# Attention plus gated MLP on one core: two-pass output tiles for three chunks, GpSimd normalising six token tiles, 128-query units in the whole last chunk, 45 exponential slots

## The chip, the cores and the metric

The kernel runs on one core of a Trainium2 chip. The core has five engines with a queue each, every queue in order: TensorE (PE in the profile; its weight loads are PEld), VectorE (DVE), ScalarE (ACT), GpSimd (POOL) and SyncE (SP), which here only issues DMAs. The metric is the device time of one execution in microseconds, the median of several runs. Before the change it is 1200.54 us (three runs: 1199.99, 1200.54 and 1211.0).

## The reference

```python
x = A_x                                   # (1, 2048, 512) bf16
xn = layernorm(x)                         # no scale, no shift, eps 1e-5
q, k, v = split(xn @ wqkv)                # 32 heads of 16
p = softmax(q @ k.T / 4)                  # per head, 2048 x 2048
attn = (p @ v) @ wo
h = silu(xn @ w1) * (xn @ w3)             # 512 -> 1792
out = x + attn + h @ w2
```

There are 32 × 2048 × 2048 scores, 134 million. Each is computed twice in this kernel: once with queries on the partitions, for the maximum of its row, and once with keys on the partitions, for the exponential.

## The kernel before

**Tiling.** The 2048 queries are four chunks of 512 (`qc` 0 to 3), the 32 heads are eight groups of four (`g`). A pair (qc, g) is worked in units of queries: 256 each as a rule, `UNIT_HEAD = (128, 128, 256)` for the first pair, and four of 128 for each of the last four pairs (`NTAIL = 4`). A unit goes through these stages:

1. *Maximum.* For each 128 queries and each pair of heads and each 512 keys, TensorE writes two banks of 512 scores (L1037), and VectorE reduces the 1024 columns to two maxima (`tensor_reduce`, L1079). There are 1024 such reduces in the kernel, eight for 128 queries; banks 0 to 3 make two places for them, so at most two are under way.
2. *Final maximum.* GpSimd merges the partial maxima in six small steps (L1187 to L1194); for the first three and the last eight units VectorE does it in one (L1216). The negative maximum becomes two rows beside Q: in most units over a DMA transpose (L1210) and two small DMAs (L1206), in the first eight units and the last four pairs over two matmuls and an evacuation (`tile_QT2`, L796; `FAST_AUG`).
3. *Exponentials.* TensorE writes the transposed scores, 512 columns to a bank (L1303), and ScalarE writes exp to a slot of 512 columns in SBUF (`PT`, L1316; two banks at once at L1346). A unit of 256 queries takes 32 slots, one of 128 takes 16; `PT` has `NPT = 39`.
4. *Values.* `tile_PV` multiplies with V and a column of ones (L567), which frees the slots. ScalarE evacuates (`U`, L1411), and a chain normalises: DMA `Lc` (L1432), reciprocal on GpSimd (L1436), DMA to DRAM and back, broadcast (L1441, L1445), multiplication on GpSimd (L1456). One chain runs at a time, and PV of unit u waits for the chain of unit u−2 (`pv_ready`). The last three units (`FAST_PV`) take a reciprocal and a product on VectorE instead (L1401, L1403).

**MLP.** `ffn_pair` makes one slice of 128 of the 1792 hidden columns for one chunk: two matmul groups, three evacuations on ScalarE (L837, L839, L843), three operations on GpSimd (L821, L824, L826) into a slot of `hT`. There are 14 slices in a chunk, 56 in all; `NHT = 24` slots, whose first four hold V's weights until V is done, and the next 16 the normalised x until it is transposed. A slice waits until the slot it takes has been read.

**Output.** `tile_OUT` adds in one bank x (identity matmul), 14 products of `hT` with w2, and 8 of the attention output with wo. For chunks in `TWO_PASS` (only chunk 2) the 14 products make a tile of their own (`tile_OUTP`), evacuated to `osb` by ScalarE and added again through an identity matmul (`g_b`) in `tile_OUT`. The last chunk has its own pair of tiles, `tile_OUTA` and `tile_OUTB`.

**Head.** x is loaded in groups of two or four token tiles (of 128 tokens). A group's statistics are taken on VectorE or ScalarE (`STATS`), two small operations on GpSimd make 1/sigma (L621, L624), and the group is normalised by VectorE (L641) or ScalarE (L637, after a small product on VectorE, L629), as `NORM` says, one letter for each of seven groups: tiles 0-1, 2-3, 4-5, 6-7, 8-11, 12-13, 14-15. The letter "p" would give it to GpSimd (`poolq["nx"]`, L647). Then a transpose and an evacuation (L672) make `xnT`, and four tiles give K of the first group for 512 keys (L688).

**Order of the work.** A planner (`while True` at L1876) walks through all engines at build time, and always places the operation that by its own table of costs can start earliest, with rules for what TensorE takes next. Each engine then runs its list in that order; only semaphores hold it back on the chip. In `later_dma` a DMA is booked with 2.3 us to landing unless told otherwise; a normalisation on GpSimd is booked with 2.08 us (L647). `ffn_from` paces the MLP slices over the reduces (from reduce −60 to reduce 600 of 1024).

Of the kernel before, what the change touches and what calls it, by code (L numbers as in the profile page):

```python
# [6 lines left out]
BF16 = mybir.dt.bfloat16  # L7
# [235 lines left out]
def _c_act(n):  # L243
    return n / 1200.0 + 0.05
# [14 lines left out]
def _build(nc, A_x, A_wqkv, A_wo, B_w1, B_w3, B_w2, out):  # L259
# [33 lines left out]
    DMA_RATE = 360.0  # L293
    NOW = 2
    FAST_HEAD = 8
    FAST_TR = 896
    DVE_HEAD = 3
# [53 lines left out]
    def sb(name, shape, dt):  # L351
        return ctx.enter_context(nc.sbuf_tensor(name, list(shape), dt))

    with ctx:
        PT = sb("PT", [128, NPT, 512], BF16)
        x_sb = PT[:, 0:NT, :]
        xr = sb("xr", [128, NXR, D], BF16)
        osb = sb("osb", [128, 4, D], BF16)
        mv = sb("mv", [128, NT, 2], FP32)
        lnr = sb("lnr", [128, NT], FP32)  # L360
        lnb = sb("lnb", [128, NT], FP32)
# [95 lines left out]
        def later_dma(fn, reads, writes, lat=2.3, cb=None, pred=None, occ=0.62):  # L457
            spq.append(_Item(fn, reads, writes, occ, lat, cb, pred))
# [25 lines left out]
        LN_GROUPS = ((0, 2), (2, 4), (4, 6), (6, 8), (8, 12), (12, 14), (14, 16))  # L484
        XN_KEYS = [("hT", DC + t) for t in range(NT)]
        xn_sb = hT[:, DC:DC + NT, :]
        landed = [DMA_FIRST]
        kb_sum = [0]

# [260 lines left out]
        def tile_V(t, need=None):  # L750
            groups = []
            for c in range(DC):
                groups.append((lambda bk, c=c: all_groups(
                    bk, xnT[:, c, t * 128:(t + 1) * 128], wv[:, c, :], D,
                    start=c == 0, stop=c == DC - 1), WV_KEYS + [("xnT", t)], _c_mm(512), None))

            def evac(bk):
                return [_Item(lambda e: e.activation(Vaug[:, t, :, 0:16],  # L758
                                                     bank(bk).rearrange("p (h d) -> p h d", d=16), ACTF.Identity),
                              [("ps", bk)], [("V", t)], _c_act(512), cb=lambda op: done.add(("V", t)))]  # L760
            return _Tile("V%d" % t, groups, evac, need=need, pred=lambda: ("xnT", t) in done)

        ug_last = {}
# [46 lines left out]
        def ffn_pair(sc, fc):  # L810
# [47 lines left out]

            def start_g():
                if idx + 2 < NQC * FC:  # L860
# [9 lines left out]
        def g_x(tg, stop=False):  # L870
            return (lambda bk: all_groups(bk, ident[:, :], xr[:, tg % NXR, :], D, start=True, stop=False),
                    [("ident",), ("xr", tg % NXR)], _c_mm(512), None)

        def g_h(tg, fc, stop=False, start=False):
            qc, ts = divmod(tg, 4)
            hs = hslot(qc * FC + fc)
            return (lambda bk: all_groups(bk, hT[:, hs, ts * 128:(ts + 1) * 128], w2[:, fc, :], D,
                                          start=start, stop=stop),
                    [("hT", hs), ("w2",)], _c_mm(512), None)
# [6 lines left out]
                    lambda: ("ON", qc, g, ts) in done)  # L886

        def store(tg):
            later_dma(lambda e: e.dma_start(out_v[:, tg, :], osb[:, tg % 4, :]), [("osb", tg % 4)], [("out", tg)],
                      cb=lambda op: done.add(("ST", tg)))  # L890

        def tile_OUT(tg):
            qc, ts = divmod(tg, 4)
            two = qc in TWO_PASS
            groups = [g_x(tg)] + ([g_b(ts)] if two else [g_h(tg, fc) for fc in range(FC)])
            groups += [g_on(qc, ts, g, False, g == NG - 1) for g in range(NG)]

            def evac(bk):
                def cb(op):
                    store(tg)  # L900
                    done.add(("OUT", tg))
                    done.add(("HP", tg))
                    if tg + NXR < NT:
                        load_xr(tg + NXR)
                return [_Item(lambda e: e.activation(osb[:, tg % 4, :], bank(bk), ACTF.Identity),
                              [("ps", bk)], [("osb", tg % 4)], _c_act(512), cb=cb)]
            return _Tile("OUT%d" % tg, groups, evac, pred=lambda: ("xr", tg) in done
                         and (("HP", tg) in done if two else (tg < 4 or ("ST", tg - 4) in done)
                              and all(("hT", qc * FC + fc) in done for fc in range(FC)))
                         and all(("ON", qc, g, ts) in done for g in range(NG)), paced=True)  # L910

        def g_b(ts):
            return (lambda bk: all_groups(bk, ident[:, :], osb[:, ts, :], D, start=False, stop=False),
                    [("ident",), ("osb", ts)], _c_mm(512), None)

        def tile_OUTP(tg):
            qc, ts = divmod(tg, 4)
            groups = [g_h(tg, fc, fc == FC - 1, fc == 0) for fc in range(FC)]

            def evac(bk):  # L920
                return [_Item(lambda e: e.activation(osb[:, ts, :], bank(bk), ACTF.Identity),
                              [("ps", bk)], [("osb", ts)], _c_act(512), cb=lambda op: done.add(("HP", tg)))]
            return _Tile("OUTP%d" % tg, groups, evac, pred=lambda: (tg < 4 or ("ST", tg - 4) in done)
                         and all(("hT", qc * FC + fc) in done for fc in range(FC)), paced=P_PACED)

        def tile_OUTA(tg):
# [15 lines left out]
        def tile_OUTB(tg):  # L942
            qc, ts = divmod(tg, 4)
            groups = [g_on(qc, ts, g, g == NGA, g == NG - 1) for g in range(NGA, NG)]

            def evac(bk):
                def cb(op):
                    store(tg)
                    done.add(("OUT", tg))
                return [_Item(lambda e: e.tensor_tensor(osb[:, tg % 4, :], bank(bk), opart[ts], ALU.add),  # L950
                              [("ps", bk)] + OP_KEYS[ts], [("osb", tg % 4)], _c_dve(512), cb=cb)]
            return _Tile("OUTB%d" % tg, groups, evac, pred=lambda: ("OUTA", tg) in done and ("ST", tg - 4) in done)


        def split_rows(u):
# [306 lines left out]
        def p2_cand():  # L1262
# [27 lines left out]
            def emit():  # L1290
# [20 lines left out]
                def cb(op):  # L1311
# [2 lines left out]
                    exp_unit[u] += 1  # L1314
                    exp_emitted.add((u, kb, j))
                expq.append(_Item(lambda e: e.activation(PT[:, sl, :], bank(b), ACTF.Exp, scale=SCALE),  # L1316
                                  [("ps", b)], [("PT", sl)], _c_act(512), cb=cb, exp=(b, sl, (u, kb, j))))
            return st, emit, rd

        def exp_pair(x, y):  # L1320
# [19 lines left out]
            def cb(op):  # L1340
# [4 lines left out]
                n_pair[0] += 1  # L1345
            return _Item(lambda e: e.activation(PT[:, s0:s1 + 1:s1 - s0, :], ps8[:, b0:b1 + 1:b1 - b0, :], ACTF.Exp,  # L1346
                                                scale=SCALE),
                         [("ps", b0), ("ps", b1)], [("PT", s0), ("PT", s1)], _c_act(1024), cb=cb)
        n_pair = [0]


# [3 lines left out]
        def tile_PV(u):  # L1355
# [5 lines left out]
            for kt in range(NT):  # L1361
# [16 lines left out]
                    return f  # L1378

                def reads(kb=kb, kt=kt):  # L1380
                    return ([("V", kt), ("Vone",), ("ones_t",)] + [("PT", pt_slot[(u, kb, j)]) for j in range(4)])

                def gcb(kb=kb, i0=i0):
                    if i0 == kpb - 1:
# [33 lines left out]
        def nrm_next():  # L1418
# [11 lines left out]

            def n1(op=None):
                later_dma(lambda e: e.dma_start(Lc[:, pp, 0:nl], U[16:128:32, us, 0:nq]), [("U", us)], [("Lc", pp)],  # L1432
                          cb=n2)
# [5 lines left out]

            def n3(op):  # L1440
                later_dma(lambda e: e.dma_start(rd_[pp][0:4 * nq].rearrange("(p n) -> p n", n=nl), Rc[:, pp, 0:nl]),  # L1441
                          [("Rc", pp)], [("rd", pp)], cb=n4)

            def n4(op):
                later_dma(lambda e: e.dma_start(  # L1445
                    R[:, pp, 0:nq], rd_[pp][0:4 * nq].rearrange("(j q) -> j q", q=nq).unsqueeze(1)
                    .broadcast_to([4, 32, nq])), [("rd", pp)], RK, cb=n5)

            def n5(op):
                nrm_busy[0] = False  # L1450
# [506 lines left out]
```

## Time and profile before

| | |
|---|---|
| median of three runs | 1200.54 us |
| the profiled execution's own time | 1199.56 us |
| its span in the trace | 1197.8 us |
| TensorE clock granted | 0.999 |
| VectorE busy | 1180.1 us (99%) |
| ScalarE busy | 1174.2 us (98%) |
| TensorE busy | 1116.0 us (93%) |
| GpSimd busy | 439.9 us (37%) |

In the profile "L1079" is a line of the kernel, "part<-ps" says that the tile `part` is written and `ps` read. Busy is the union of the instructions' spans: an engine that pipelines looks full when its instructions overlap at their ends, so a busy share near 100% is not yet proof of a full engine. "Idle before" is how long the engine stood before the instructions of a group, and the name behind the arrow is what released it. The timeline merges equal neighbours: start, length, engine, line, operation, names, shapes, count.

### The profile page before, as it was taken

What the parts mean: (1) busy time and instruction counts of PE and PEld (TensorE: products, weight loads), DVE (VectorE), ACT (ScalarE), POOL (GpSimd) and SP (SyncE); (2) the same over time, 40 slices, a digit from 0 to 9 for tenths busy, and PEclk for the clock granted to TensorE, in tenths of its full rate; (3) what the DMA queues carried; (4) which work ended last, traced back from release to release, by engine and by line L of the source; (5) the groups of instructions that cost most, each with busy time, mean ns of one, the idle gap of its engine ahead of it and who ended that gap; (6) DMA issues with size and microseconds to landing.
All of it is one profiled execution on the core that took longest, in us unless ns stands there. A gap on an engine that the chain in (4) does not pass through costs nothing.

```text
span 1197.8 us, 32744 instructions
## 1 busy us (share of the span) xinstructions
PE 1116.0 (93%) x13564; PEld 467.9 (39%) x13731; DVE 1180.1 (99%) x1087; ACT 1174.2 (98%) x2272; POOL 439.9 (37%) x854
## 2 busy tenths in 40 slices
PE   8999999999999999998999999999999999889998
PEld 3433333333334433333333333433333343345554
DVE  8999999999999999999999999999999999999995
ACT  7899999999999999999999999999999999999997
POOL 2254555645222256642222243265632122233220
PEclk9999999999999999999999999999999999999999
DMA  6422223222001122210001121022100200000000
GB/s 185 124 59 72 52 64 81 48 55 52 19 23 29 41 54 50 61 29 20 22 16 33 31 59 29 22 64 45 40 20 20 59 22 19 18 18 14 12 12 23
DMA packets 128321, 51.41 MB, mean 43 GB/s; under 512 B 97252, under 2 KB 128172, under 8 KB 128172
## 3 DMA queue, kind: packets, MB, share of 16 engines
q1 hardware_dynamic: 128172, 49.30, 16.3%
q8 instruction: 108, 1.77, 0.6%
q14 instruction: 41, 0.34, 0.1%
HBM read 38.86 MB, written 6.74 MB: 38 GB/s over the span
## 4 chain that ended last, share of the span: by engine, by line
DVE 44%; ACT 27%; PE 25%; issue 3%; POOL 1%; DMA 1%; another core or an unknown queue 0%; POOLq 0%
DVE part L1079 43%; ACT PT L1316 19%; PE ps L581 9%; PE ps L1303 7%; PE ps L567 5%; PE ps L1037 4%; ACT PT L1346 3%; ACT th L837 1%; ACT zg L839 1%; ACT ub L843 1%; ACT U L1411 1%; ACT xnT L672 0%; ACT kq L743 0%; ACT Vaug L758 0%; DMA R<-rd 0%
## 5 line engine op out<-in xcount | busy, mean ns | idle before, releaser
L1079 DVE TENSOR_REDUCE part<-ps 128x2 f32<-128x1024 f32 x1024 | 1159.9, 1212 | 0.7 <-PE ps L1303 0.4
L1316 ACT ACTIVATE PT<-ps 128x512 bf16<-128x512 f32 x1750 | 922.4, 627 | 5.7 <-PE ps L1303 2.5
L1303 PE MATMUL ps<-QT,KT 32*128 32x256 bf16 (+1 forms) x4672 | 538.0, 259 | 11.7 <-ACT PT L1346 6.0
L1037 PE MATMUL ps<-KT,QT 32*128 32x512 bf16 x2048 | 400.7, 384 | 12.5 <-DVE part L1079 7.9
L1303 PEld LDWEIGHTS ps<-QT,KT 32*128 32x128 bf16 x4672 | 204.3, 92 | 224.8 <-issue 96.9
L581 PE MATMUL ps<-xnT,ident 128*128 128x512 bf16 (+1 forms) x599 | 174.6, 348 | 23.0 <-ACT PT L1346 7.0
L1436 POOL TENSOR_TENSOR Rc<-Lc,mone 128x8 f32<-128x8 f32 (+1 forms) x70 | 106.0, 1514 | 228.0 <-DMA Lc<-U 228.0
L567 PE MATMUL ps<-PT,Vaug 128*17 128x256 bf16 (+1 forms) x4672 | 175.2, 261 | 4.5 <-ACT zg L839 1.3
L581 PE MATMUL ps<-xnT,w 128*128 128x512 bf16 (+1 forms) x550 | 146.1, 334 | 13.0 <-ACT zg L839 5.7
L1346 ACT ACTIVATE PT<-ps 128x1024 bf16<-128x1024 f32 x149 | 151.7, 1050 | 0.8 <-PE ps L1303 0.5
L1037 PEld LDWEIGHTS ps<-KT,QT 32*128 32x128 bf16 x2048 | 98.1, 91 | 131.5 <-DVE part L1079 66.6
L567 PEld LDWEIGHTS ps<-PT,Vaug 128*17 128x17 bf16 x4672 | 86.5, 89 | 78.0 <-issue 57.6
L581 PEld LDWEIGHTS ps<-xnT,ident 128*128 128x128 bf16 x700 | 52.3, 97 | 107.7 <-ACT PT L1316 47.7
L824 POOL TENSOR_TENSOR a<-zg,ub 128x512 f32<-128x512 bf16 x56 | 64.6, 1153 | 44.7 <-ACT ub L843 44.3
L1187 POOL TENSOR_TENSOR mx<-part 128x16 f32<-128x16 f32 (+1 forms) x62 | 13.2, 212 | 179.1 <-DVE part L1079 179.0
L581 PEld LDWEIGHTS ps<-xnT,w 128*128 128x128 bf16 x578 | 44.2, 97 | 84.2 <-issue 47.0
L826 POOL TENSOR_TENSOR hT<-a,t 128x512 bf16<-128x512 f32 x56 | 71.0, 1269 | 2.6
L581 PE MATMUL ps<-w,hT 128*128 128x256 bf16 (+1 forms) x270 | 68.7, 336 | 2.6 <-issue 1.1
L1456 POOL TENSOR_TENSOR wk_on<-U,R 128x256 bf16<-128x256 f32 (+1 forms) x37 | 23.4, 632 | 118.0 <-DMA R<-rd 118.0
L1456 POOL TENSOR_TENSOR on_b<-U,R 128x256 bf16<-128x256 f32 (+1 forms) x33 | 23.4, 710 | 71.1 <-DMA R<-rd 71.1
L839 ACT ACTIVATE zg<-ps 128x512 bf16<-128x512 f32 x56 | 36.3, 649 | 0.0
L843 ACT ACTIVATE ub<-ps 128x512 bf16<-128x512 f32 x56 | 35.9, 641 | 0.0
(89 smaller groups left out, 520.8 us busy)
## 6 DMA issues: line engine op xcount, KB each, us to landing
w<-in_B_w_dram SPq DMA_DIRECT2D x112, 128.0 KB
R<-rd SPq DMA_DIRECT2D x55, 128.0 KB
QT<-qd SPq DMA_DIRECT2D x31, 128.0 KB
KT<-kd SPq DMA_DIRECT2D x28, 128.0 KB
xr<-in_A_x_dram SPq DMA_DIRECT2D x16, 128.0 KB
out_dram<-osb SPq DMA_DIRECT2D x16, 128.0 KB
qd<-kq SPq DMA_DIRECT2D x15, 128.0 KB
w<-in_B_w_dram SPq DMA_DIRECT2D x1, 1792.0 KB
```

The lines of the kernel that those rows point to most:

```text
L567: ins = e.matmul(bank(bk)[32 * i:32 * i + m, c0 + a:c0 + b], make_lhsT(i), rhs if (a, b) == (0, ncols) else rhs[:, a:b], start=start, stop ...
L581: return e.matmul(bank(bk)[0:rows, c0 + a:c0 + b], lhsT, rhs if (a, b) == (0, ncols) else rhs[:, a:b], start=start, stop=stop, **kw)
L824: q.append(_Item(lambda e: e.tensor_tensor(a32[:, :], zg[:, ss, :], ub[:, ss, :], ALU.mult), [("zg", ss), ("ub", ss)], [("a32",)], 1.1, 1.25))
L826: q.append(_Item(lambda e: e.tensor_tensor(hT[:, hslot(idx), :], a32[:, :], t1[:, :], ALU.mult), [("a32",), ("t1",)], [("hT", hslot(idx))] ...
L839: _Item(lambda e: e.activation(zg[:, ss, :], bank(bk), ACTF.Identity, scale=0.5), [("ps", bk)], [("zg", ss)], _c_act(512), cb=part_done, n ...
L843: return [_Item(lambda e: e.activation(ub[:, ss, :], bank(bk), ACTF.Identity), [("ps", bk)], [("ub", ss)], _c_act(512), cb=part_done)]
L1037: ins = e.matmul(bank(2 * sl + i), QT[32 * j:32 * j + 32, qs, q * 128:(q + 1) * 128], KT[32 * j:32 * j + 32, g, c_ * 512:(c_ + 1) * 512], ...
L1079: redq.append(_Item(lambda e: e.tensor_reduce(dst, pair_ap.rearrange("p (a b) -> p a b", b=512), AX.X, ALU.max), writes, [("part", par, qt ...
L1303: ins = e.matmul(bank(b)[:, i * nq:(i + 1) * nq], KT[32 * j:32 * j + 32, g, (k0 + i) * 128:(k0 + i + 1) * 128], QT[32 * j:32 * j + 32, qs, ...
L1316: expq.append(_Item(lambda e: e.activation(PT[:, sl, :], bank(b), ACTF.Exp, scale=SCALE), [("ps", b)], [("PT", sl)], _c_act(512), cb=cb, e ...
L1346: return _Item(lambda e: e.activation(PT[:, s0:s1 + 1:s1 - s0, :], ps8[:, b0:b1 + 1:b1 - b0, :], ACTF.Exp, scale=SCALE), [("ps", b0), ("ps ...
L1436: poolq["nrm"].append(_Item(lambda e: e.tensor_tensor(Rc[:, pp, 0:nl], Lc[:, pp, 0:nl], mone[:, 0:nl], ALU.pow), [("Lc", pp), ("mone",)], ...
```

## The change

Five edits come together.

1. `TWO_PASS = (0, 1, 2)`: the output tiles of chunks 0 and 1 are made in two passes as well. `osb`, the buffer of both passes, grows from 4 to 8 tiles (`NOSB`).
2. `hT` becomes a part of the same SBUF tensor as `PT`, with 20 slots in place of 24. The four that hold V's weights become exponential slots when V is done, beside `NPT = 41`: 45 in all in place of 39. The MLP keeps 16 slots, and a slice waits for the two-pass tile of the chunk that had its slot before.
3. `NORM`: tiles 8 to 11 go from VectorE to GpSimd, tiles 12 and 13 from ScalarE to GpSimd.
4. `NTAIL = 8`: all eight pairs of the last chunk are worked in units of 128 queries (before, the last four).
5. The planner books the three DMAs of the normalising chain with 2.6, 2.6 and 2.9 us in place of 2.3.

```diff
-    NPT = 39
+    NPT = 41
-    TWO_PASS = (2,)
+    TWO_PASS = (0, 1, 2)
-    NHT = 24
+    NHT = 20
-    NTAIL = 4
+    NTAIL = 8
+    NOSB = 8
+    LAT_L = 2.6
+    LAT_D = 2.6
+    LAT_R = 2.9
-    NORM = "dddddaa"
+    NORM = "ddddppa"
...
-        PT = sb("PT", [128, NPT, 512], BF16)
+        PT = sb("PT", [128, NPT + NHT, 512], BF16)
-        osb = sb("osb", [128, 4, D], BF16)
+        osb = sb("osb", [128, NOSB, D], BF16)
-        hT = sb("hT", [128, NHT, 512], BF16)
+        hT = PT[:, NPT:NPT + NHT, :]
...
+        def v_done(t):
+            done.add(("V", t))
+            if all(("V", t_) in done for t_ in range(NT)):
+                pt_free.extend(range(NPT, NPT + DC))
...
         def hslot(idx):
-            return (idx + DC) % NHT
+            return DC + idx % (NHT - DC)
...
                 if idx < NHT - DC:
                     return True
-                if idx < NHT:
-                    return all(("V", t) in done for t in range(NT))
-                return all(("HP", (idx - NHT) // FC * 4 + ts) in done for ts in range(4))
+                return all(("HP", (idx - NHT + DC) // FC * 4 + ts) in done for ts in range(4))
...
-            groups = [g_x(tg)] + ([g_b(ts)] if two else [g_h(tg, fc) for fc in range(FC)])
+            groups = [g_x(tg)] + ([g_b(tg)] if two else [g_h(tg, fc) for fc in range(FC)])
...
                 later_dma(lambda e: e.dma_start(Lc[:, pp, 0:nl], U[16:128:32, us, 0:nq]), [("U", us)], [("Lc", pp)],
-                          cb=n2)
+                          lat=LAT_L, cb=n2)
```

In the rest of the diff `osb` is indexed by `tg % NOSB` in place of `tg % 4` or `ts`, the keys of slots above `NPT` are those of `hT`, and the other two DMAs of the chain get `LAT_D` and `LAT_R`.

More of the change, by code (lines that the diff above doesn't have):

```diff
@@ L888, in store @@
         def store(tg):
-            later_dma(lambda e: e.dma_start(out_v[:, tg, :], osb[:, tg % 4, :]), [("osb", tg % 4)], [("out", tg)],
+            later_dma(lambda e: e.dma_start(out_v[:, tg, :], osb[:, tg % NOSB, :]), [("osb", tg % NOSB)], [("out", tg)],
                       cb=lambda op: done.add(("ST", tg)))
@@ L920, in evac @@
             def evac(bk):
-                return [_Item(lambda e: e.activation(osb[:, ts, :], bank(bk), ACTF.Identity),
-                              [("ps", bk)], [("osb", ts)], _c_act(512), cb=lambda op: done.add(("HP", tg)))]
-            return _Tile("OUTP%d" % tg, groups, evac, pred=lambda: (tg < 4 or ("ST", tg - 4) in done)
+                return [_Item(lambda e: e.activation(osb[:, tg % NOSB, :], bank(bk), ACTF.Identity),
+                              [("ps", bk)], [("osb", tg % NOSB)], _c_act(512), cb=lambda op: done.add(("HP", tg)))]
+            return _Tile("OUTP%d" % tg, groups, evac, pred=lambda: (tg < NOSB or ("ST", tg - NOSB) in done)
                          and all(("hT", qc * FC + fc) in done for fc in range(FC)), paced=P_PACED)
@@ L949, in cb @@
                     done.add(("OUT", tg))
-                return [_Item(lambda e: e.tensor_tensor(osb[:, tg % 4, :], bank(bk), opart[ts], ALU.add),
-                              [("ps", bk)] + OP_KEYS[ts], [("osb", tg % 4)], _c_dve(512), cb=cb)]
-            return _Tile("OUTB%d" % tg, groups, evac, pred=lambda: ("OUTA", tg) in done and ("ST", tg - 4) in done)
+                return [_Item(lambda e: e.tensor_tensor(osb[:, tg % NOSB, :], bank(bk), opart[ts], ALU.add),
+                              [("ps", bk)] + OP_KEYS[ts], [("osb", tg % NOSB)], _c_dve(512), cb=cb)]
+            return _Tile("OUTB%d" % tg, groups, evac, pred=lambda: ("OUTA", tg) in done and ("ST", tg - NOSB) in done)
         def split_rows(u):
@@ L1380, in reads @@
                 def reads(kb=kb, kt=kt):
-                    return ([("V", kt), ("Vone",), ("ones_t",)] + [("PT", pt_slot[(u, kb, j)]) for j in range(4)])
+                    return ([("V", kt), ("Vone",), ("ones_t",)] + [pt_key(pt_slot[(u, kb, j)]) for j in range(4)])
                 def gcb(kb=kb, i0=i0):
```

24 lines of the change are left out of this document (13 added, 11 removed).

## The prediction

> **What bounds the kernel now.** I read the page's busy shares first, then the groups, then the timelines of single engines at both ends. Busy shares and the costliest group of the kernel before:
>
> ```profile
> span 1197.8 us, 32744 instructions
> PE 1116.0 (93%) x13564; PEld 467.9 (39%) x13731; DVE 1180.1 (99%) x1087; ACT 1174.2 (98%) x2272; POOL 439.9 (37%) x854
> L1079 DVE TENSOR_REDUCE part<-ps 128x2 f32<-128x1024 f32 x1024 | 1159.9, 1212 | 0.7 <-PE ps L1303 0.4
> ```
>
> 1024 reduces take 1159.9 us, 1.133 us each, and VectorE stood 0.7 us before all of them together. ScalarE looks as full, but it isn't. Its two groups of exponentials on the page, a stretch of its timeline late in the kernel, and its two sizes of U evacuation and the two-pass evacuation among the groups:
>
> ```profile
> L1316 ACT ACTIVATE PT<-ps 128x512 bf16<-128x512 f32 x1750 | 922.4, 627 | 5.7 <-PE ps L1303 2.5
> L1346 ACT ACTIVATE PT<-ps 128x1024 bf16<-128x1024 f32 x149 | 151.7, 1050 | 0.8 <-PE ps L1303 0.5
> ...
> 1020.38 6.09 ACT L1316 ACTIVATE PT<-ps 128x512 bf16<-128x512 f32 x12
> L1411 ACT ACTIVATE U<-ps 128x256 f32<-128x256 f32 x55 | 21.4, 389 | 0.5 <-PE ps L567 0.5
> L1411 ACT ACTIVATE U<-ps 128x128 f32<-128x128 f32 x15 | 4.3, 286 | 0.0
> L921 ACT ACTIVATE osb<-ps 128x512 bf16<-128x512 f32 x4 | 2.5, 624 | 0.0
> ```
>
> Twelve exponentials in 6.09 us are some 0.50 us each when they overlap, so the 2048 need at most 1024 us. With the other 100 us of its busy time (1174.2 less 922.4 and 151.7) ScalarE needs about 1125 us of the 1160 that VectorE works. It follows; VectorE leads. So the time is three pieces: what comes before the first reduce, the reduces with whatever VectorE does between them, and what comes after the last. VectorE's timeline, head and tail:
>
> ```profile
> 14.10 0.68 DVE L608 BATCH_NORM_STATS2 t<-PT 128x6 f32<-128x512 bf16 x1
> 14.82 1.38 DVE L641 TENSOR_SCALAR hT<-PT,mv,lnr 128x512 bf16<-128x512 bf16 x4
> 16.12 0.24 DVE L611 BATCH_NORM_AGGREGATE mv<-t 128x2 f32<-128x6 f32 x2
> 16.28 2.32 DVE L1079 TENSOR_REDUCE part<-ps 128x2 f32<-128x1024 f32 x2
> 18.51 0.15 DVE L629 SCALAR_TENSOR_TENSOR lnb<-mv,lnr 128x2 f32<-128x2 f32 x1
> 18.58 5.95 DVE L1079 TENSOR_REDUCE part<-ps 128x2 f32<-128x1024 f32 x5
> 24.45 0.15 DVE L629 SCALAR_TENSOR_TENSOR lnb<-mv,lnr 128x2 f32<-128x2 f32 x1
> ...
> 1169.05 6.87 DVE L1079 TENSOR_REDUCE part<-ps 128x2 f32<-128x1024 f32 x6
> 1176.57 0.96 DVE L1401 RECIPROCAL R<-ps 128x128 f32<-128x128 f32 x1 [0.66 <-PE ps L567]
> 1177.57 0.29 DVE L1403 TENSOR_TENSOR wk_on<-ps,R 128x128 bf16<-128x128 f32 x1
> 1177.78 1.21 DVE L1079 TENSOR_REDUCE part<-ps 128x2 f32<-128x1024 f32 x1
> ```
>
> The first reduce starts at 16.28, the last ends at 1178.99 (1177.78 + 1.21), the span at 1197.8: 16.3 + 1162.7 + 18.8 us. An edit can only pay by what it takes from the first or last piece, or from the 2.8 us by which the middle exceeds the reduces. Anything it takes from ScalarE, TensorE or GpSimd in the middle is worth nothing.
>
> **The change part by part.**
>
> *Normalising on GpSimd.* On VectorE's path four instructions go: from 14.82 to the next start at 16.12, 1.30 us. The small product of tiles 12 and 13 goes too (18.51 to 18.58, 0.07 us). Was a reduce waiting behind them? TensorE and GpSimd there:
>
> ```profile
> 14.07 0.39 PE L1037 MATMUL ps<-KT,QT 32*128 32x512 bf16 x4 [0.48 <-ACT QT L778]
> 13.77 1.01 POOL L624 TENSOR_TENSOR lnr<-lnt,mhalf 128x4 f32<-128x4 f32 x1
> 16.72 0.70 POOL L624 TENSOR_TENSOR lnr<-lnt,mhalf 128x2 f32<-128x2 f32 x1
> ```
>
> The scores of two reduces (four matmuls) were written by 14.46, so the first reduce can follow the statistics that end at 14.78. First reduce about 14.9, gain 1.30 + 0.07 = 1.4 us. A wait takes the place of the removed work: the transposes of tiles 8 to 13 now wait for GpSimd, TensorE and ScalarE queue behind them in order, and K of keys 1024 to 2047 comes later. The nearest prices of one normalisation on GpSimd, and the rows that it must meet:
>
> ```profile
> L821 POOL TENSOR_SCALAR t<-th 128x512 f32<-128x512 bf16 x56 | 34.8, 622 | 3.0 <-POOL hT L826 1.3 <-ACT th L837 0.4 <-ACT PT L1316 0.2
> L826 POOL TENSOR_TENSOR hT<-a,t 128x512 bf16<-128x512 f32 x56 | 71.0, 1269 | 2.6
> 23.64 0.79 ACT L688 ACTIVATE KT<-ps,kbias 128x512 bf16<-128x512 f32 x1
> 25.03 1.51 ACT L637 ACTIVATE hT<-PT,lnb,lnr 128x512 bf16<-128x512 bf16 x2
> 30.58 0.69 ACT L688 ACTIVATE KT<-ps,kbias 128x512 bf16<-128x512 f32 x1 [0.69 <-PE ps L581]
> ```
>
> The same operation with constants takes 0.62 us, a two-input one 1.27; the planner books 2.08 (L647). I bound it by 0.62 and 3.3 us (below) and take the planner's 2.08 as the careful value. Tiles 8 to 11 then leave GpSimd at 14.8 + 4 × 2.08 + 0.9 for another group's sigma = 24.0, and K of the third 512 keys about 4 us later (transposes, evacuations, four matmuls, evacuation), 28 in place of 24.4. Who waits? The first three units have 16 reduces on the first 1024 keys: 16 × 1.133 = 18.1 us from 14.9, so VectorE has work until 33. Tiles 12 and 13 leave at 28.2; the last K comes about 31.5, against 31.3 now, where tiles 14 and 15 on ScalarE (25.03) set it. Eight reduces on the third K carry VectorE to 42. So the cover is 5 us, and it is gone when a normalisation costs over 2.08 + 5/4 = 3.3 us. ScalarE is relieved of two normalisations, 1.51 us, off the path.
>
> On the Trainium skill's page "GPSIMD Engine Reference" § 3.1 one-input work costs about 1.8 cycles an element at 1.2 GHz: an estimate by it of 0.77 us for 512, beside the trace's 0.62 of the like row. By that price the cover would be larger, the sum the same.
>
> *Two passes for chunks 0 and 1.* Eight more evacuations on ScalarE (8 × 0.62 = 5.0 us) and eight more identity matmuls. Neither is on the path: ScalarE has the 35 us worked out above, TensorE reached the reduces in time all through. Slices of the MLP are no longer held back at chunk borders, so ScalarE's and GpSimd's load is spread evenly until about reduce 600 and ends earlier. VectorE waited at no border, so nothing is gained either. Value 0; if ScalarE's slack were gone, 5 us.
>
> *45 slots.* More room for ScalarE to run ahead of the values. By the 0.7 us of idle time, ScalarE never held VectorE up. Value 0, in the tail between 0 and the gain under the rivals.
>
> *128-query units in the first half of the last chunk.* 16 units in place of 8, off VectorE's path: GpSimd takes their final maximum (all but the last eight units). ScalarE pays 16 × 0.286 − 8 × 0.389 = 1.5 us. SP issues one transpose, two small DMAs and the three of the chain for each, now every 8 × 1.133 = 9.06 us. SP's and GpSimd's rows for one chain of a 256 unit beside a transpose, and one of a 128 unit without:
>
> ```profile
> 892.49 0.58 SPq L1432 DMA_DIRECT2D Lc<-U  x1
> 900.75 0.73 POOL L1456 TENSOR_TENSOR on_b<-U,R 128x256 bf16<-128x256 f32 x1 [4.72 <-DMA R<-rd]
> 906.53 1.21 SPq L1210 DMA_TRANSPOSE Zs<-Z  x1
> 909.35 1.09 SPq L1206 DMA_DIRECT2D QT<-Zs  x2
> ...
> 1076.69 0.53 SPq L1432 DMA_DIRECT2D Lc<-U  x1
> 1084.19 0.46 POOL L1456 TENSOR_TENSOR wk_on<-U,R 128x128 bf16<-128x128 f32 x1 [4.02 <-DMA R<-rd]
> ```
>
> The mixture, a 128 unit with a transpose, isn't in the trace. The chain took 9.0 us (892.49 to 901.48) and 8.0 us. PV of unit u waits for the chain of u−2, so PV, its evacuation and one chain must fit into two units, 18.1 us; with 9.0 for the chain and about 3.5 for PV, 12.5 do. SP's issues are some 3.7 of 9.06 us. Value 0. From below a gain isn't excluded, since units half as large let exponentials start after 9 in place of 18 us, but no row shows that VectorE waits for them; from above it is the second rival.
>
> *Booked DMA times.* They change only the order. No instruction is added; 0.
>
> **Sum.** 1199.56 (the profiled execution's own time; 1.76 around the span of 1197.8) − 1.4 = 1198.2. The median is 0.98 above that execution, so 1199.1 us. 1% of this kernel, 12 us, is about what a measurement can tell from no change.
>
> **The rivals.**
>
> *The tail gets shorter.* Before the last reduce VectorE ran a reciprocal and a product of PV and waited 0.66 us for them: from 1175.92 to 1177.78, 1.9 us on the path. ScalarE's first and last exponentials of the last unit:
>
> ```profile
> 1181.63 1.02 ACT L1346 ACTIVATE PT<-ps 128x1024 bf16<-128x1024 f32 x1
> 1191.54 0.60 ACT L1316 ACTIVATE PT<-ps 128x512 bf16<-128x512 f32 x1
> ```
>
> 16 exponentials took 10.5 us where 16 × 0.50 = 8.0 would do. A new order could save both, 4.4 us: 1194.7. For it: slots and PV's places change just there. Against: the last four pairs keep their units, their way over `tile_QT2` and their three fast PVs. 0.14.
>
> *The normalising chain falls behind (the slower side).* In the first half of the last chunk SP serves two chains of dependent DMAs in one queue: a DMA that waits for GpSimd's reciprocal holds the transpose of the next unit behind it, and the other way round. If these waits add over 18.1 − 12.5 = 5.6 us to a pair of units, PV falls back, slots run out, and exponentials pile up beyond the last reduce. One and a half units of them, 24 × 0.50 = 12 us: 1211. Against: the chain beside a transpose took 9.0 us, and most of SP's time there is idle. 0.11.
>
> *VectorE starves in the head.* If a normalisation takes, say, 4 us, the third K is (4 − 3.3) × 4 = 2.8 us too late, and the last one (six tiles) a few more: gain gone, 1199.1 + 5 = 1204. Against: both GpSimd rows are far below. 0.08.
>
> *A small VectorE instruction is locked out.* The remaining product of tiles 14 and 15 (L629) reads two SBUF tiles; it would now meet a normalisation. Were it to wait for one to end, up to 2.1 us of the 1.4 gained are lost: up to 1201.2, about 1200.2. The trace has no GpSimd instruction beside either L629. 0.05.
> The Trainium skill's page "SBUF — State Buffer" § Who interferes with whom states such a rule: a VectorE instruction with two SBUF inputs and a GpSimd one that reads SBUF exclude each other for a whole instruction, while a reduce never takes the shared pair. No run here shows it yet.
>
> *The edit moves nothing*, another wait taking the 1.4 us: 1200.5, inside the forecast's own range. 0.05.
>
> **How the numbers follow.** Forecast 0.57, 1199.1, own range 1197 to 1201.5. The 80% range leaves out the chain rival (0.11) and the ends of the others: 1194.0 to 1206.0. Faster by over 1% would need 12 us, while the head gives 1.4 and the tail 4.4: 0.01. Slower by over 1% is the upper part of the chain rival and what I didn't see: 0.08. Within 1%: 0.91.
>
> **What would show it.** In VectorE's timeline the first reduce near 14.9, no L641 beyond tile 7, and one L629. The reduces' idle time still about 1 us; above 3 us I am wrong on the head or on the order. GpSimd rows of L641's operation near 14.8 to 28 give their price. The last reduce should end near 1177.6, with 18 to 19 us of span behind it; a tail over 22 us means the chain rival, under 16 the shorter tail. The MLP's rows should end near 700 us (reduce 600 × 1.133 us + 16). What makes it wrong: a plan that puts TensorE's score matmuls behind something late for long, which no row of before can show.

## The result

The changed kernel takes 1197.18 us (median of 22 runs, 1196.7 to 1199.87), the kernel before beside it 1200.01 us (22 runs): 2.8 us faster, a ratio of 0.9968 with a 95% interval of 0.9955 to 0.9981. That is clear of zero and far below 1%. The time fell inside the forecast's own range (1197 to 1201.5), at its fast end; 1.4 us of gain were forecast. Some executions lose 1.5 to 8 us while the granted TensorE clock stands at half (for 6.8 us in one profile below, for 20.5 us in another); the ones without such a drop are called undisturbed.

The page of the changed kernel; its lines are numbered 10 to 12 higher than before (the reduce is L1089, GpSimd's and VectorE's normalisation L653):

```profile
span 1195.2 us, 34930 instructions
PE 1122.1 (94%) x14546; PEld 495.0 (41%) x14711; DVE 1178.8 (99%) x1082; ACT 1171.8 (98%) x2324; POOL 466.5 (39%) x940
L1089 DVE TENSOR_REDUCE part<-ps 128x2 f32<-128x1024 f32 x1024 | 1160.1, 1210 | 0.8 <-PE ps L1047 0.7
```

The reduces cost what they did, and VectorE stood 0.8 us before them. VectorE's timeline of the changed kernel at both ends:

```profile
14.07 0.69 DVE L620 BATCH_NORM_STATS2 t<-PT 128x6 f32<-128x512 bf16 x1
14.67 0.16 DVE L623 BATCH_NORM_AGGREGATE mv<-t 128x2 f32<-128x6 f32 x1
14.75 1.19 DVE L1089 TENSOR_REDUCE part<-ps 128x2 f32<-128x1024 f32 x1
...
23.96 0.15 DVE L641 SCALAR_TENSOR_TENSOR lnb<-mv,lnr 128x2 f32<-128x2 f32 x1
...
36.64 0.17 DVE L1226 TENSOR_REDUCE negm<-part 128x4 f32<-128x16 f32 x1
...
1174.59 0.94 DVE L1411 RECIPROCAL R<-ps 128x128 f32<-128x128 f32 x1
1175.57 0.29 DVE L1413 TENSOR_TENSOR wk_on<-ps,R 128x128 bf16<-128x128 f32 x1
1175.78 1.22 DVE L1089 TENSOR_REDUCE part<-ps 128x2 f32<-128x1024 f32 x1
```

The first reduce starts at 14.75 (16.28 before), the last ends at 1177.00 (1178.99), the span at 1195.2. So the three pieces are 14.75 + 1162.25 + 18.2 us, against 16.28 + 1162.71 + 18.81: 1.5 us from the head, 0.5 from the middle (the reciprocal at 1174.59 no longer waits 0.66 us) and 0.6 from the tail.

Two other rows of the changed kernel: GpSimd's price for a normalisation, and when ScalarE starts its exponentials:

```profile
L653 POOL TENSOR_SCALAR PT<-PT,mv,lnr 128x512 bf16<-128x512 bf16 x6 | 12.4, 2075 | 0.3
```
```profile
32.25 0.69 ACT L700 ACTIVATE KT<-ps,kbias 128x512 bf16<-128x512 f32 x1 [1.77 <-PE ps L593]
38.61 0.27 ACT L808 ACTIVATE QT<-ps 128x128 bf16<-128x128 f32 x1
39.42 1.02 ACT L1356 ACTIVATE PT<-ps 128x1024 bf16<-128x1024 f32 x1 [0.54 <-PE ps L1313]
```

The first exponentials come at 39.4 us. The last K lands at 32.9, and the first unit's final maximum is at 36.64, where before it was at 34.82. The head helps VectorE and makes ScalarE late; whether the second matters is what the experiments had to settle. The first reduce itself isn't exact to better than about 0.9 us: in the ten profiles below with this share of the normalisation it starts between 14.66 and 15.56, as VectorE waited 1.6 to 2.4 us for x.

### The profile page after: what moved, and what is told of

Its sections match the earlier page's. It is cut to its first block, busy times and chain, and to the rows that moved or that the text cites. A ratio compares the mean times of both kernels' runs of the same rounds, so it can differ in the third digit from the quotient of the medians.

```text
span 1195.2 us, 34930 instructions
## 1 busy us (share of the span) xinstructions
PE 1122.1 (94%) x14546; PEld 495.0 (41%) x14711; DVE 1178.8 (99%) x1082; ACT 1171.8 (98%) x2324; POOL 466.5 (39%) x940
## 4 chain that ended last, share of the span: by engine, by line
ACT 47%; PE 36%; DVE 14%; issue 2%; DMA 0%; POOL 0%; SPq 0%; POOLq 0%
ACT PT L1326 35%; DVE part L1089 13%; PE ps L593 12%; PE ps L1313 11%; PE ps L579 8%; ACT PT L1356 5%; PE ps L1047 5%; ACT th L849 2%; ACT zg L851 1%; ACT U L1421 1%; ACT ub L855 1%; ACT kq L755 1%; DMA PT<-in_A_x_dram 0%; PE ps L677 0%; ACT QT L808 0%
## 5 line engine op out<-in xcount | busy, mean ns | idle before, releaser
L1089 DVE TENSOR_REDUCE part<-ps 128x2 f32<-128x1024 f32 x1024 | 1160.1, 1210 | 0.8 <-PE ps L1047 0.7
L1326 ACT ACTIVATE PT<-ps 128x512 bf16<-128x512 f32 x1826 | 958.8, 643 | 2.1 <-PE ps L1313 0.9
L1313 PE MATMUL ps<-QT,KT 32*128 32x256 bf16 (+1 forms) x5184 | 564.9, 249 | 10.1 <-ACT PT L1356 5.8
L1313 PEld LDWEIGHTS ps<-QT,KT 32*128 32x128 bf16 x5184 | 234.0, 92 | 235.8 <-issue 96.9
L579 PE MATMUL ps<-PT,Vaug 128*17 128x256 bf16 (+1 forms) x5184 | 180.5, 252 | 4.5 <-ACT zg L851 1.5
L593 PE MATMUL ps<-xnT,ident 128*128 128x512 bf16 (+1 forms) x540 | 158.4, 345 | 20.3 <-ACT PT L1356 4.6
L1356 ACT ACTIVATE PT<-ps 128x1024 bf16<-128x1024 f32 x111 | 114.8, 1062 | 1.2 <-PE ps L1313 1.0
L593 PEld LDWEIGHTS ps<-xnT,ident 128*128 128x128 bf16 x617 | 46.5, 96 | 86.5 <-ACT PT L1326 43.4
L593 PE MATMUL ps<-w,PT 128*128 128x512 bf16 (+1 forms) x268 | 70.1, 332 | 3.3 <-ACT U L1421 1.6
L838 POOL TENSOR_TENSOR PT<-a,t 128x512 bf16<-128x512 f32 x56 | 70.9, 1266 | 2.9
L1466 POOL TENSOR_TENSOR wk_on<-U,R 128x128 bf16<-128x128 f32 (+1 forms) x45 | 24.8, 551 | 66.3 <-DMA R<-rd 66.3
```

The source lines that it names most:

```text
L579: ins = e.matmul(bank(bk)[32 * i:32 * i + m, c0 + a:c0 + b], make_lhsT(i), rhs if (a, b) == (0, ncols) else rhs[:, a:b], start=start, stop ...
L593: return e.matmul(bank(bk)[0:rows, c0 + a:c0 + b], lhsT, rhs if (a, b) == (0, ncols) else rhs[:, a:b], start=start, stop=stop, **kw)
L838: q.append(_Item(lambda e: e.tensor_tensor(hT[:, hslot(idx), :], a32[:, :], t1[:, :], ALU.mult), [("a32",), ("t1",)], [("hT", hslot(idx))] ...
L1089: redq.append(_Item(lambda e: e.tensor_reduce(dst, pair_ap.rearrange("p (a b) -> p a b", b=512), AX.X, ALU.max), writes, [("part", par, qt ...
L1313: ins = e.matmul(bank(b)[:, i * nq:(i + 1) * nq], KT[32 * j:32 * j + 32, g, (k0 + i) * 128:(k0 + i + 1) * 128], QT[32 * j:32 * j + 32, qs, ...
```

## The experiments

The first theory is the prediction's: VectorE leads, ScalarE follows with slack. After the first four runs a second one stands beside it: ScalarE is as full as VectorE, and what it leaves idle shows at the end. The runs come from three chips, each with runs of the kernel before beside them (1199.35, 1199.94 and 1200.13 us); a difference to the changed kernel's 1197.2 us, which was measured beside 1200.01, can hold up to 0.7 us of that.

**The normalisation alone, and everything but it.**

```diff
-    NORM = "dddddaa"
+    NORM = "ddddppa"
```

> The kernel before with one edit: GpSimd normalises tiles 8 to 13. Theory (VectorE leads, and the head's four normalisations stood ahead of the first reduce): first reduce at 14.8 us in place of 16.3, the rest unchanged to 0.5 us, 1.5 us faster than before, about 1198.5 us. Rival (the gain sits in the other edits: slots, two passes, small units): within 0.5 us of before, whatever the first reduce does.

Measured: median 1197.29 us beside a before of 1199.35. Eight of twelve executions lie between 1195.9 and 1197.6. The other four, the profiled one among them, are at 1203.5 to 1205.0, with a mean TensorE clock of 0.99; the ratio over all is therefore 0.9996 (0.998 to 1.0011). In undisturbed executions the edit brings about 2.3 us, more than the 1.5 expected. The first reduce came at 14.91 us. Only a disturbed execution was profiled, so where the other 0.9 us come from isn't shown.

```diff
-    NORM = "ddddppa"
+    NORM = "dddddaa"
```

> The changed kernel with tiles 8 to 11 back on VectorE and 12 and 13 back on ScalarE. Theory: first reduce back at 16.3 us, 1.5 us slower than the changed kernel, 1198.7 us, still 1.3 us faster than before through the tail and the middle. Rival: the other edits carry all of it, 1197.2 us.

Measured: 1197.64 us, ratio 0.9987 (0.9978 to 0.9995) to before. Undoing it costs 0.5 us against the changed kernel's 1197.2, or 1.1 when each is taken against the kernel before beside it, not 1.5. The first reduce went back to 16.62 us as expected, and the last one ends at 1179.1, 2.1 us later than in the changed kernel: VectorE pays the head in full. But the tail is 17.3 us in place of 18.2. ScalarE's first exponential also moved, to 37.1 us, 2.3 us earlier; that isn't what shortens the tail, for by 80 us this kernel has finished 64 exponentials (counted in 512 columns) and the changed one 65, and both have 21 left when the last reduce ends. What differs is the time after the last exponential, 6.3 against 7.4 us. In the changed kernel TensorE runs eight products of the output (1187.98 to 1189.87) before the last 32 products with V; in this one they come behind them.

**More work for ScalarE.** Each evacuation of the up projection twice:

```diff
+                        _Item(lambda e: e.activation(ub[:, ss, :], bank(bk), ACTF.Identity),
+                              [("ps", bk)], [("ub", ss)], _c_act(512)),
                         _Item(lambda e: e.activation(ub[:, ss, :], bank(bk), ACTF.Identity),
                               [("ps", bk)], [("ub", ss)], _c_act(512), cb=part_done)]
```

> The changed kernel with each of the 56 evacuations of the up projection done twice on ScalarE: 56 x 0.50 us = 28 us more of ScalarE, in the first 800 us. Theory (ScalarE has some 35 us of slack behind its 98% of busy time): no change, 1197 to 1199 us, fewer gaps between exponentials. Rival (ScalarE's 98% is real, it bounds the kernel beside VectorE): 28 us less the 23 us of its idle time outside the middle that cannot be used, so 1220 to 1225 us.

Measured: 1223.0 us, 1.0196 (1.0183 to 1.0209). The first theory fails: of the 28 us (an estimate, from 0.50 us each) 26 come out at the end by the median, 23 in the fastest of the four executions (1220.44). The rival's range holds, but not by its own sum, since 28 less 23 would have been 5; the runs fit 28 paid nearly whole. VectorE's timeline of this kernel at its end:

```profile
1168.87 8.01 DVE L1091 TENSOR_REDUCE part<-ps 128x2 f32<-128x1024 f32 x7
1176.91 0.17 DVE L1228 TENSOR_REDUCE negm<-part 128x4 f32<-128x16 f32 x1
...
1201.44 0.96 DVE L1413 RECIPROCAL R<-ps 128x128 f32<-128x128 f32 x1 [23.94 <-PE ps L579]
1210.23 0.96 DVE L1413 RECIPROCAL R<-ps 128x128 f32<-128x128 f32 x1 [5.95 <-PE ps L579]
1217.91 0.96 DVE L1413 RECIPROCAL R<-ps 128x128 f32<-128x128 f32 x1 [5.18 <-PE ps L579]
```

VectorE finished its reduces at 1176.9, where it does in the changed kernel. Then it stood 23.9 us until values arrived: ScalarE had fallen behind by that much, unseen in VectorE's idle time. When the last reduce ended, 69 exponentials were left, 21 in the changed kernel: 48 × 0.50 = 24 us.

**More work for VectorE.** One reduce in 64 twice:

```diff
+                if n % 64 == 32:
+                    redq.append(_Item(lambda e: e.tensor_reduce(
+                        dst, pair_ap.rearrange("p (a b) -> p a b", b=512), AX.X, ALU.max),
+                        writes, [("part", par, qt, j, c_) for j, c_ in cells], _c_dve(1024)))
```

> The changed kernel with 16 of the 1024 reduces done twice on VectorE, one in 64: 16 x 1.133 = 18.1 us. Theory (VectorE leads all the way): 1197.2 + 18.1 = 1215.3 us, to 1 us. Rival (another engine leads in part of the middle, and VectorE follows it): under 1208 us.

Measured: 1217.62 us (1.0155, 1.0142 to 1.0168): 20.4 us more than the changed kernel, all of the 18.1 and some; above the 1215.3 ± 1 expected, and far from the rival's 1208. VectorE's time is paid in full.

**Less work for ScalarE.** The gate's linear part is left out:

```diff
-                if cnt[0] < 3:
+                if cnt[0] < 2:
...
-                        _Item(lambda e: e.activation(zg[:, ss, :], bank(bk), ACTF.Identity, scale=0.5),
-                              [("ps", bk)], [("zg", ss)], _c_act(512), cb=part_done, name="glue")]
```

> The changed kernel without the 56 evacuations of the gate's linear part; the MLP multiplies the tanh with the up projection instead, so its hidden values are not the reference's: 28 us less of ScalarE work. Second theory (VectorE and ScalarE both full, each sets a lower bound): VectorE's last reduce stays at 1177 us, ScalarE has nothing left over after it but the last unit, and only the tail shrinks, from 18.2 us to some 16: 1194 to 1196 us. Rival (ScalarE alone is the bound): 10 us or more faster. First theory (VectorE alone): no change beyond 0.5 us.

Measured: 1196.55 us beside 1200.13 before (0.9972, 0.9962 to 0.9983). Against the changed kernel's 1197.2 that is 0.6 us, from 28 us less work, so ScalarE alone isn't the bound. But VectorE's last reduce didn't stay at 1177. Its longest waits for scores, and its timeline at the end:

```profile
DVE part L1087 <- PE ps L1045: 2.2, 2, 1.9
```
```profile
1170.24 3.49 DVE L1087 TENSOR_REDUCE part<-ps 128x2 f32<-128x1024 f32 x3 [1.89 <-PE ps L1045]
...
1174.83 4.61 DVE L1087 TENSOR_REDUCE part<-ps 128x2 f32<-128x1024 f32 x4
```

The tail shrank from 18.2 to 15.7 us, with only the 16 exponentials of the last unit left, as the second theory has it. The last reduce ends at 1179.4, 2.4 us later: the first one started 0.4 us later, and reduces waited 2.4 us for scores in place of 0.7, 1.9 us of it just before the end. So more ScalarE work costs nearly its full length; less can only shorten the tail, here by 2.5 us, and VectorE gave that back. Whether it had to, or the planner's new order happened to cost it, isn't shown.

**The changed kernel again, and its edits undone one by one.** First itself:

> The changed kernel itself, as the reference for this chip and these runs. Both theories: 2.8 us faster than before, 1196.5 us beside a kernel before of 1199.35.

Measured: median 1198.59 us beside 1199.94 (0.9986, 0.9977 to 0.9995). Four of eleven executions are at 1197.0 to 1197.4, the rest at 1198.5 to 1199.7 with a clock of 0.996 to 0.997. The gain here is 1.4 us by medians, 2.8 us in the undisturbed ones.

```diff
-    NTAIL = 8
+    NTAIL = 4
```

> The changed kernel with 128-query units in the last four pairs only. First theory (VectorE alone leads): no change, within 0.4 us of the changed kernel. Second theory (ScalarE is as full as VectorE and what it leaves idle shows at the end): 8 evacuations fewer, 1.5 us less ScalarE work, 0 to 1.5 us faster. Rival (the small units carry the gain, their exponentials start 9 us after the maxima begin in place of 18): 1 to 2.5 us slower.

Measured: 1198.85 us (0.9992, 0.9983 to 1.0001). By medians 0.3 us slower than the changed kernel on that chip; against its undisturbed executions 1.3 to 1.8. The interval doesn't decide; a gain from leaving the small units out, as the second theory had it, wasn't seen. In its profile 22 exponentials are left at the last reduce, 21 in the changed kernel, so what it lost it lost before the tail.

```diff
-    NPT = 41
+    NPT = 35
```

> The changed kernel with 39 exponential slots in place of 45 (35 and the four of V). First theory: within 0.4 us. Second theory: ScalarE's idle time between 40 and 1180 us goes from 2.6 us back towards the 7.3 us of before, and the kernel is 1 to 4 us slower with the last reduce where it was and a longer tail.

Measured: 1198.42 us (0.9985, 0.9976 to 0.9994), equal to the changed kernel's median there, 1.3 us above its undisturbed executions. In its profile the last reduce ends at 1175.1, 1.9 us earlier than in the changed kernel, and the span at 1196.9: the tail grew from 18.2 to 21.7 us, with 28 exponentials left in place of 21. ScalarE's idle time from 40 to 1178 us grew only from 2.4 to 4.8. The place of the cost is as expected, its size smaller.

```diff
-    TWO_PASS = (0, 1, 2)
+    TWO_PASS = (2,)
```

> The changed kernel with two passes in chunk 2 only, the 16 slots of the MLP kept. First theory: within 0.4 us. Second theory: ScalarE has 8 evacuations less (4 us), but the MLP waits at chunk borders again, so that its evacuations come in lumps: between 2 us faster (the work counts) and 4 us slower (the lumps count).

Measured: 1205.43 us (1.0046, 1.0032 to 1.0059), 6.8 us slower than the changed kernel's median on that chip and over the 4 us allowed. Busy time by stretch (columns: stretch, its length, busy us and instructions of PE, PEld, DVE, ACT and POOL, granted clock, DMA share, GB/s), first of the changed kernel, then of this one:

```profile
500.00:600.00 100.00, 95.97 (x1006) 38.63 (x1018) 99.50 (x89) 99.67 (x202) 52.48 (x89) 1.00 0.17 40
600.00:700.00 100.00, 96.09 (x1034) 38.40 (x1044) 100.00 (x89) 99.80 (x202) 39.06 (x70) 1.00 0.18 45
```
```profile
500.00:600.00 100.00, 89.19 (x1082) 33.55 (x1095) 100.00 (x89) 99.23 (x179) 26.61 (x62) 1.00 0.09 23
600.00:700.00 100.00, 93.91 (x1082) 36.39 (x1095) 100.00 (x90) 96.26 (x180) 23.74 (x54) 1.00 0.13 34
900.00:1000.00 100.00, 95.10 (x1514) 49.11 (x1531) 100.00 (x90) 100.00 (x208) 47.53 (x122) 1.00 0.16 38
```

VectorE runs at its pace in both. ScalarE's counts, 202 and 202 against 179 and 180, must be read with care: 28 and 14 of the latter write 1024 columns at once (L1356), 5 and 4 of the former. Counted in 512 columns that is 207 and 206 against 207 and 194. What differs is the kind of work. No up projection is evacuated here between 218 and 411 us and between 501 and 694 us, where the MLP waits at a chunk border; the kernel before has two such gaps as well (293 to 426 and 523 to 706 us), and in the changed kernel the longest is 71 us. From 200 to 700 us ScalarE evacuates 52 MLP banks, 105 in the changed kernel, and makes up for these 53 with only 38 more exponentials (900 against 862). The rest falls due after 700 us, and ScalarE can't catch up: the last reduce ends at 1176.1 with 43 exponentials left, the span at 1203.7, a tail of 27.5 us. This is with 16 slots for the MLP; the kernel before, with one pass, had 24. What the run shows is that 16 slots need the two passes; 24 slots beside the other edits weren't run.

```diff
-    LAT_L = 2.6
-    LAT_D = 2.6
-    LAT_R = 2.9
+    LAT_L = 2.3
+    LAT_D = 2.3
+    LAT_R = 2.3
```

> The changed kernel with the planner's 2.3 us for the three DMAs of the normalising chain. Only the order changes. Second theory: within 1.5 us of the changed kernel on either side, by what ScalarE idles. Rival (the booked times are what makes the small units work): over 3 us slower, with a longer tail.

Measured: 1202.0 us (1.0014, 1.0005 to 1.0023), 3.4 to 4.9 us slower than the changed kernel (its median and its undisturbed executions on another chip): the rival's number, and only in part its reason. The tail is 19.9 us, 1.7 longer. More went before it: the last reduce ends at 1181.3, 4.3 us later. VectorE's waits in this kernel, and two stretches of it:

```profile
DVE part L1089 <- PE ps L1313: 3.1, 5, 1.3
DVE part L1089 <- PE ps L1047: 1.7, 3, 0.9
```
```profile
880.00:900.00 20.00, 18.02 (x196) 6.61 (x196) 18.88 (x18) 18.29 (x28) 5.70 (x18) 0.91 0.09 25
1040.00:1060.00 20.00, 17.36 (x340) 9.37 (x330) 17.56 (x17) 17.47 (x35) 6.04 (x20) 0.91 0.05 10
```

Of the 4.8 us that VectorE waited for scores, some 1.1 and 2.4 lie in these two stretches, where the granted clock was 0.91, and 1.00 in the changed kernel. All eleven executions had a clock of 0.995 to 0.999. That the booked times place TensorE's work so that its clock drops is the reading nearest to the rows; the order differs everywhere, so it isn't proved.

**Two other shares for the head.** Tiles 12 and 13 back on ScalarE, and on VectorE:

```diff
-    NORM = "ddddppa"
+    NORM = "ddddpaa"
```

> The changed kernel with tiles 12 and 13 back on ScalarE, tiles 8 to 11 on GpSimd. Second theory: VectorE loses 0.07 us; the last K no longer waits for GpSimd's fifth and sixth tile, so the first unit's maximum is done about 35 us in place of 36.7 and ScalarE starts its exponentials 1.5 us earlier, in a stretch where it stood 7 us idle: 0.5 to 1.5 us faster than the changed kernel. First theory: no change.

Measured: 1195.76 us (five runs) beside 1200.13 (0.9965, 0.9952 to 0.9977): 4.4 us faster than before by medians, where the changed kernel was 2.8. It is the fastest kernel of this study; its interval overlaps the changed kernel's. The rows of its head:

```profile
30.57 0.69 ACT L700 ACTIVATE KT<-ps,kbias 128x512 bf16<-128x512 f32 x1 [0.60 <-PE ps L593]
37.24 0.28 ACT L808 ACTIVATE QT<-ps 128x128 bf16<-128x128 f32 x1 [0.48 <-PE ps L593]
38.17 1.08 ACT L1326 ACTIVATE PT<-ps 128x512 bf16<-128x512 f32 x2
```

The last K and the first exponential are 1.7 and 1.3 us earlier than in the changed kernel, and both this and the gain are as the second theory had them. But its rows don't join the two: the head start is gone by 80 us (66 exponentials finished, 65 in the changed kernel), and 22 are left at the last reduce, 21 there. The last reduce ends 0.2 us earlier; the rest of the gain is the time after the last exponential, 6.0 in place of 7.4 us. So the number was right, its reason wasn't seen.

```diff
-    NORM = "ddddppa"
+    NORM = "ddddpda"
```

> The changed kernel with tiles 12 and 13 on VectorE, tiles 8 to 11 on GpSimd. First theory: VectorE pays 2 x 0.33 us, 0.65 us slower than the changed kernel. Second theory: the same price on VectorE, but ScalarE starts its exponentials up to 2 us earlier: between 1 us faster and 0.3 us slower.

Measured: 1197.66 us (0.9979, 0.997 to 0.9988), 0.5 us slower than the changed kernel. Both theories were allowed nearly this, so the run tells little between them. ScalarE starts 0.7 us earlier (38.73), and again 21 exponentials are left at the last reduce, which ends 1.9 us later than in the changed kernel; the tail is 1.4 us shorter. The run shows something else, at the end.

## Why the prediction was right, and where it was not

*The sum.* 1199.1 was forecast, 1197.2 measured: right in direction, half of the size. That it lies in the range owes something to luck. The term of the head was right, and the four edits valued at 0 weren't nothing, but came to little together.

*The head.* Right in its steps. First reduce 14.9 forecast, 14.75 measured; one L641 is left; GpSimd's normalisation takes 2.08 us, exactly what the planner booked, and not near the rows of 0.62 and 1.27 us with constants or two tensors. The 0.77 us estimated beside it from the Trainium skill's page "GPSIMD Engine Reference" § 3.1, whose 1.8 cycles are a best case, is off by a factor of 2.7. VectorE never starved: the third and the last K landed at 28.9 and 32.9 us (28 and 31.5 forecast), before it needed them. That the first exponential would come 2.6 us later (39.4, before 36.8) the prediction didn't say; it did no harm, for by 80 us the two kernels have finished 65 and 64 exponentials.

*ScalarE's slack.* "ScalarE needs about 1125 us of the 1160 that VectorE works" is the step that failed. The other 100 us came from subtracting two groups from the busy total; but the total is a union of spans, and the groups overlap in it. The three MLP groups alone show it in the changed kernel:

```profile
L851 ACT ACTIVATE zg<-ps 128x512 bf16<-128x512 f32 x56 | 37.3, 667 | 0.0
L855 ACT ACTIVATE ub<-ps 128x512 bf16<-128x512 f32 x56 | 37.2, 664 | 0.0
L849 ACT ACTIVATE th<-ps 128x512 bf16<-128x512 f32 x56 | 36.6, 654 | 0.0
```

111 us, already more than the 100 that were left for everything. These are spans again, so they are too much as the 100 are too little. Taken from one start to the next in the trace before, and priced by the median of each kind, the 373 instructions that aren't exponentials need some 160 us (30 of them before the first exponential) and the exponentials some 1000: 1160 us in place of 1125. This is an estimate, and it leaves a little room; that there is next to none is what the runs show. What they left for after the last reduce, by the traces (exponentials in 512 columns; times in us):

| kernel | exponentials left | last exponential after last reduce | end after that | tail |
|---|---|---|---|---|
| before | 26 | 13.2 | 5.7 | 18.8 |
| changed | 21 | 10.8 | 7.4 | 18.2 |
| 28 us more ScalarE work | 69 | 40.3 | 5.4 | 45.7 |
| 28 us less | 16 | 10.1 | 5.6 | 15.7 |
| 39 slots | 28 | 16.3 | 5.4 | 21.7 |
| two passes in chunk 2 only | 43 | 22.1 | 5.4 | 27.5 |
| tiles 8 to 13 back | 21 | 11.0 | 6.3 | 17.3 |
| tiles 12 and 13 back on ScalarE | 22 | 11.2 | 6.0 | 17.2 |

VectorE's idle time shows none of this. The last unit alone is 16, so the changed kernel is five behind. Against the kernel before its ScalarE is 2.4 us nearer to the last reduce, and 1.7 us of that are lost again after the last exponential.

*Edits valued at 0.* This followed from that step. Added up from the kernel before, in undisturbed executions beside it, the head's edit alone brings 2.3 us, the other four without it 1.7, all together 2.8: they don't add, and on top of the head the four bring about 0.5. Undone one at a time, the two passes cost 6.8 to 8.3 us, the booked times 3.4 to 4.9, the slots and the small units 0 to 1.8 each, the normalisation 0.5 to 1.1. These add up to far more than 2.8, so they aren't shares of the gain. "VectorE waited at no border, so nothing is gained" looked at the wrong engine: at a border the MLP's work on ScalarE stops, and the debt is paid in the tail.

One rival was left standing throughout. Each edit makes the planner order the whole kernel anew, and no run holds the order fixed. From the first to the last reduce the changed kernel and the variants without a drop of the clock (and with 1024 reduces) take 1160.3 to 1164.3 us, a spread of which the instructions that an edit adds to VectorE there explain at most 1.3 us. So a difference of 1 or 2 us between two variants can be the order's; the 6.8 us of the two passes and the 23 to 26 us of the added ScalarE work are beyond it.

*Booked DMA times.* "They change only the order; 0" was right in its first half. Undoing it cost more than undoing any other edit but one, by a way that isn't proved.

*The rivals.* The shorter tail came in part: 0.6 us, and 0.5 by the reciprocal that no longer waits, of the 4.4. Of these 4.4, 2.5 were never there: between the two rows that the prediction shows (1181.63 and 1192.14) ScalarE wrote 21 exponentials of 512 columns, not 16, at 0.50 us each. The chain rival didn't appear: with the small units the tail is 18.2 us. The locked-out product didn't appear in the changed kernel (0.15 us at 23.96, while GpSimd normalised from 23.21 on). The MLP's last row is at 773.7 us, not 700. The spans gained 2.6 us; the 1.2 beyond the forecast are these 1.1 of the middle and the tail, and 0.1 of the head.

## What to carry to other kernels

A busy share is a union of spans; taking one union from another doesn't give the time that the rest needs, and here the 98% was nearer the truth than the correction. To learn an engine's slack, price its work from start to start, column for column (one instruction can write two banks), or give it more work and see. An engine that the bound engine never waits for may still have no slack: its debt appears after the bound engine's last instruction, so count what is left there. Where an edit makes an engine late or early in the head, follow it: here 1.3 to 2.6 us were gone by 80 us, and a gain that looked like theirs lay in what came after the last exponential.

## What the runs showed that was not expected

**The TensorE clock.** One stretch of the changed kernel's repeat, whose granted clock was 0.996 overall:

```profile
190.00:200.00 10.00, 9.26 (x85) 3.47 (x88) 9.58 (x10) 9.55 (x19) 6.46 (x13) 0.92 0.41 107
200.00:210.00 10.00, 9.66 (x99) 3.37 (x90) 8.49 (x8) 7.73 (x16) 3.23 (x5) 0.73 0.16 35
```

The clock lost 0.8 and 2.7 us in two slices: it is granted 0.50 from 198.5 to 205.3 us, for 6.8 us, and VectorE stood 1.9 us. The same program ran elsewhere without it. The Trainium skill's page "TensorE: Matmul & The Clock Gate" § Part 1 says that the clock is halved after an idle window of 3.4 us, whose phase is free; 6.8 us are two such windows, and the trace agrees with half speed and with chance between executions. It doesn't show an idle window: in the 3.4 us before the drop TensorE was busy 84% of the time, with no gap above 0.54 us in the 15 us before, so by busy share no one would look for one there.

**GpSimd beside VectorE.** In the kernel with tiles 12 and 13 on VectorE, GpSimd's timeline and VectorE's:

```profile
20.46 2.25 POOL L653 TENSOR_SCALAR PT<-PT,mv,lnr 128x512 bf16<-128x512 bf16 x1
23.41 2.07 POOL L653 TENSOR_SCALAR PT<-PT,mv,lnr 128x512 bf16<-128x512 bf16 x1
```
```profile
20.52 1.01 DVE L653 TENSOR_SCALAR PT<-PT,mv,lnr 128x512 bf16<-128x512 bf16 x2
23.73 0.45 DVE L641 SCALAR_TENSOR_TENSOR lnb<-mv,lnr 128x2 f32<-128x2 f32 x1
```

VectorE's two normalisations took 1.01 us in place of 0.72, the small product 0.45 in place of 0.15, and GpSimd's normalisation 2.25 in place of 2.08. So in this profile the two engines hinder each other, as the page "SBUF — State Buffer" of the Trainium skill § Who interferes with whom states; but the loser waited 0.3 us, not for the rest of a 2.1 us instruction as that section has it, and in the eleven other profiles in which the product met a normalisation it lost nothing (0.14 or 0.15 us).
